# Key sums in two column runs, weight sums on one engine, and later output products in a fused attention and expert kernel

## The chip, the core and the metric

The kernel runs on one core of a Trainium2 chip. The core has TensorE (PE in the profile; PEld is its weight load), VectorE (DVE), ScalarE (ACT), GpSimd (POOL), SyncE (SP, which only issues transfers here) and 16 DMA engines. The metric is the time of one execution in microseconds (us) on the device. The kernel before takes 847.71 us, the median of three runs (847.57 to 850.11).

## The reference

An attention with a decay bias feeds one expert layer, and that feeds a second one. All arrays are float32.

```python
# 4 batches, 8 heads, 576 tokens, 64 wide
scores = scale * np.matmul(q, k.transpose(0, 1, 3, 2))
cum = np.cumsum(np.maximum(s, 0.0), axis=-1)
bias = -(cum[:, :, :, None] - cum[:, :, None, :])
scores = np.where(causal, -1000000000.0, scores + np.minimum(bias, 0.0))
attn = np.exp(scores - np.max(scores, axis=-1, keepdims=True))
attn = attn / (np.sum(attn, axis=-1, keepdims=True) + 1e-09)
x = np.matmul(attn, v)                       # to 2304 tokens x 512
h = np.maximum(x @ w_in, 0.0)                # first expert, 2048 wide
x = h * h @ w_out
h = np.maximum(np.maximum(x @ w1, x @ w2), x @ w3)   # second, 768 wide
return h @ w_out                             # w_out of the second expert
```

The running sum `cum` of the 32 rows of `s` (one row for each batch and head) is what the text below calls the key sums.

## The kernel before

**Setup.** The 32 rows of `s` are loaded into a tile `st`. VectorE clips and scales them (L581), scans them into running sums (L582), and cuts each sum into three bfloat16 parts that add up to it (L584 and L586, three casts with two subtractions between them). Each part goes by a small transfer into rows of two operand tiles: `ck` (three transfers from SP's queue) and `cq` (three from ACT's, L614). For the first pair of heads TensorE multiplies `xq` by `xk` (L644) and then adds `cq` by `ck` (L646) into the same bank, which puts the sums' difference into the scores. For the later pairs the parts go through `c_dram` (written at L588, read at L611). SP's queue then loads `xv` of pair 0 and all operands of the next pairs.

**Attention.** Sixteen pairs of heads run through nine units each: scores (L644 to L654), row maximum on VectorE (L667), exponential on ScalarE (L681), transposes on TensorE (L723), copies on ScalarE (L743 to L748), product with `xv` (L768). Meanwhile the expert weights, which are float64 words, are turned into two float32 halves. A job for one weight block loads its words (L392), works on them with VectorE (L397 to L408), adds two pieces (L415), rounds the high half on ScalarE (L429) and subtracts it for the low half (L433). The engine of L415 and L433 is `adder[0]`: POOL while attention runs, VectorE afterwards. `w_job` reads it once, when a job is made, so a job that begins in attention keeps POOL.

**First expert** (about 177 to 566 us). For each block of 128 hidden columns TensorE makes the hidden block (L812), ScalarE applies relu and square and rounds it (L971 to L973), VectorE makes the low half (L974), and two blocks later TensorE multiplies by `w_out` (L995).

**Second expert** (566 to 842 us). There are three groups of 768 tokens. A group has nine items, `m % PER` 0 to 8, of seven products each (L1132, places `c` 0 to 6 in an item), written so that an item's last products lie between the next item's first. ScalarE copies some product banks to tiles `s1`, `s5` and `s2` (L1033), VectorE adds others to them (L1051) and takes maxima (L1068, L1073) into `res`. After an item's last product `res` is ready; for output rows of 128 tokens `split_out` rounds it on ScalarE (L804) and takes the low half on VectorE (L807) into a tile `hh`, and `out_products` (L1104) multiplies by the second `w_out`: six such token blocks in a group, 18 products of 512 columns each, then a copy to `ob` (L1110 or L1112) and the store (L1114). `OUT2_AT` says after which item and which place of the next group each token block of the last group stands. The third group's blocks come at the end, one behind another. The order of all engines is the order of the code; weight tiles `sl` are a pool of 19, refilled from `keep_p` by SP (L504) when the last product on them is done.

Of the kernel before, what the change touches and what calls it, by code (L numbers as in the profile page):

```python
# [8 lines left out]
F32 = mybir.dt.float32  # L9
# [4 lines left out]
ALU = mybir.AluOpType  # L14
# [6 lines left out]
MAX_PAIRS = 0  # L21
PUMP_FROM = 9
PUMP_END = 0
PRE = 2
PRE_X = (30, 21, 12, 5)
PRE_AT = 1
# [17 lines left out]
FAR = 24  # L44
PACE_FAR = 3
RR = 2
OUT2_AT = {1: {0: 0, 4: 1}, 2: {1: 2, 5: 3}, 3: {0: 4, 2: 5}}
LAG = 2
MAX_OPEN = 3
ST_BUFS = 3  # L50
# [196 lines left out]
def kernel(  # L247
# [15 lines left out]
    nc = tc.nc  # L263
    P = 128
    D = v_tail.shape[2]
    S = qT.shape[2]
    H = 8
    BH = s.shape[0]
    B = BH // H
    NT, DM = out.shape  # L270
# [6 lines left out]
    NU = 2 * SQ // P + 1  # L277
# [6 lines left out]
    def f32(ap):  # L284
        return ap.bitcast(F32)
# [62 lines left out]
    T2 = 384  # L348
# [71 lines left out]
    def w_job(i, t):  # L420
        if i[0] == "P":
            return item_job(*i[1:])
        b = {}
        add = adder[0]
        first = words_of(i, b, lambda: (f32(b["a"]), add))

        def high_part():
            b["h"] = t[:, 0, :] if t is not None else sums_tile()[:, 0:512].bitcast(F32R)
            nc.scalar.copy(out=b["h"], in_=f32(b["a"]))  # L429

        def low_part():
            b["l"] = t[:, 1, :] if t is not None else b["a"].bitcast(F32R)
            add.tensor_tensor(out=b["l"], in0=f32(b["a"]), in1=f32(b["h"]), op=ALU.subtract)  # L433

        def store():
            for h, x in enumerate((b["h"], b["l"])):
                queue[0].dma_start(out=keep[i][:, h * 512:(h + 1) * 512], in_=f32(x))

        stages = first + [(high_part, 0, 0), (low_part, 1, 0.4)]
        takes, gives = {0: "st", 2: "wa"}, {6: ["st"], 8: ["wa"]}  # L440
        if t is None:
            stages += [(store, 1, 2), (lambda: None, 0, 0)]
            takes[7], gives[10], gives[8] = "sums", ["sums", "wa"], []
        return [x[0] for x in stages], takes, gives, tuple(zip(*[x[1:] for x in stages]))
# [107 lines left out]
    def setup():  # L552
# [3 lines left out]
        parts = st[2][0:BH, :].bitcast(BF16)[:, 0:3 * S].rearrange("p (r c) -> p r c", r=3)  # L556
        c8 = e_u[NU - 1][0:BH, 0:S]
        nc.sync.dma_start(out=sc, in_=s)
        k, q, cum, v = loads(0)
        k()  # L560
        q()
# [16 lines left out]
        nc.vector.memset(bound[:, 0:SQ - P], 0.0)  # L578
        nc.vector.memset(bound_l[:, 0:SQ], 0.0)
        nc.vector.memset(e_u[NU - 1][:, S:], 0.0)  # L580
        nc.vector.tensor_scalar(out=sc, in0=sc, scalar1=0.0, scalar2=8.0, op0=ALU.max, op1=ALU.mult)  # L581
        nc.vector.tensor_tensor_scan(out=c8, data0=one, data1=sc, initial=0.0, op0=ALU.mult, op1=ALU.add)  # L582
        for r in range(3):
            nc.vector.tensor_copy(parts[:, r, :], c8)  # L584
            if r < 2:
                nc.vector.tensor_tensor(out=c8, in0=c8, in1=parts[:, r, :], op=ALU.subtract)  # L586
        cum(parts)
        nc.sync.dma_start(out=c_dram, in_=parts)  # L588
        v()
        for j in range(2):  # L590
            nc.vector.tensor_copy(bound_l[rows(j), SQ:S], bound[rows(j), SQ - P + D * j:SQ - P + D * (j + 1)])

# [3 lines left out]
    def loads(p):  # L596
# [7 lines left out]
            nc.sync.dma_start(out=d["xq"], in_=qT[p])  # L604


        def cum(parts=None):
            for t, r, queue in ((ck[p % 3], 0, nc.sync), (cq[p % 3], 3, nc.sync if parts is None else nc.scalar)):
                if parts is None:
                    for j in range(2):  # L610
                        queue.dma_start(out=t[D * j + r:D * j + r + 3, :], in_=c_dram[2 * p + j])  # L611
                else:
                    for i in range(3):
                        queue.dma_start(out=t[r + i:r + i + D + 1:D, :], in_=parts[2 * p:2 * p + 2, i, :])  # L614

        def v():
            d["xv"] = hp.tile([P, 2, NKT, D], F32, tag="xv", name="xv")
# [261 lines left out]
    def experts():  # L879
# [138 lines left out]
        phS.close()  # L1018
        slots.soon_kept = SOON_KEPT_2
        with ExitStack() as ph2:  # L1020
            r_p, hh_p, c_p, s_p, o_p = (ph2.enter_context(tc.tile_pool(name=n, bufs=b, reuse_waits="tile"))
                                        for n, b in (("rr2", 2), ("hh2", 2), ("cc2", 1), ("ss2", 2), ("oo2", 2)))
            rings = dict(X=Ring(banks[0:3]), Z=Ring(banks[3:5]), Y=Ring(banks[5:6]))
            ring_o = Ring(banks[6:8])
            where = {0: "X", 1: "Z", 2: "X", 3: "Y", 4: "X", 5: "Z", 6: "X"}
# [3 lines left out]
            tmp = {}  # L1029

            def copied(m, name, bank):
                x = tmp[m, name] = s_p.tile([P, T2], F32, tag=name, name=name)
                nc.scalar.copy(out=x, in_=bank[:, 0:T2])  # L1033

            def after(m, i):
# [54 lines left out]
            def out_products(g, t, f, begin, end):  # L1090
# [5 lines left out]
                for k, (lo, hi) in enumerate(cols):  # L1096
# [8 lines left out]
                                                 start=(begin and n == h == c == 0),  # L1105
                                                 stop=(end and n == len(f) - 1 and h == 1 and c == 2))
                    if end:
                        ob = o_p.tile([P, DM], F32, tag="ob", name="ob")[:, 0:hi - lo]
                        if (t + k) % 2:
                            nc.vector.tensor_copy(ob, b)  # L1110
                        else:
                            nc.scalar.copy(out=ob, in_=b)  # L1112
                        ring_o.give(po.pop((g, t)))
                        nc.sync.dma_start(out=out[groups[g] + t * P:groups[g] + (t + 1) * P, lo:hi], in_=ob)  # L1114
# [3 lines left out]
            for item in main2:  # L1118
                if item[0] == "p":
# [23 lines left out]
                    if m == len(items) - 1 and i == 6:  # L1143
                        for t in range(2):
                            split_out(last, t, order2[-1:])
                else:
                    _, g, t, f, begin, end = item
                    out_products(g, t, f, begin, end)
                    ahead = t + (1 if g < last else 2)
                    if end and ahead < 2 * T2 // P:  # L1150
                        split_out(g, ahead, range(NQ))
                slots.pos += 1
# [64 lines left out]
```

## Time and profile before

| | |
|---|---|
| median of three runs | 847.71 us |
| the profiled execution, its own time | 847.02 us |
| its span | 845.2 us |
| TensorE busy | 826.4 us (98%) |
| VectorE, ScalarE, POOL busy | 524.3, 407.5, 175.4 us |
| granted TensorE clock | 1.00 throughout |
| attention, first expert, second expert | to 177, 177 to 566, 566 to 842 us |

The span is what the profiler saw between the first and the last instruction; 1.8 us of the execution lie around it. TensorE is busy nearly all the time, so the places to read are those where it waits, and those where the same run of products takes longer than elsewhere: the profile models the end of a matmul, so a short wait shows better in the distance between the starts than in the busy time.

### The profile page before, as it was taken

How to read it: one execution, taken by the hardware profiler on the slowest of the kernel's cores; microseconds unless marked ns; L12 is line 12 of the kernel's file. 1: busy time of each engine (PE TensorE's matmuls, PEld its weight loads, DVE VectorE, ACT ScalarE, POOL GpSimd, SP SyncE). 2: the span in 40 equal slices, each digit the busy share in tenths (PEclk: the TensorE clock that was granted, in tenths of full speed). 3: DMA queues.
4: the chain of work that ended last, by engine and by line, in shares of the span. 5: the costliest groups of instructions: out<-in, count | busy, mean ns of one | idle time of the engine just before them, and what ended most of it. 6: DMA issues, size and time to landing. Idle time of an engine off the chain costs nothing.

```text
span 845.2 us, 14494 instructions
## 1 busy us (share of the span) xinstructions
PE 826.4 (98%) x5284; PEld 700.5 (83%) x5284; DVE 524.3 (62%) x1103; ACT 407.5 (48%) x833; POOL 175.4 (21%) x273
## 2 busy tenths in 40 slices
PE   5999999999999999999999999999999999999998
PEld 3555565577888899999998888889998899899996
DVE  6777787749766656765877786843563335633442
ACT  5888889845544445445544555432242222421221
POOL 3054444544231323222123232100000000000000
PEclk9999999999999999999999999999999999999999
DMA  5565657453544454896758596639921573026602
GB/s 162 178 192 170 218 188 217 123 154 126 179 153 148 150 194 150 310 362 218 243 201 309 181 314 228 248 105 406 407 91 44 197 262 121 13 75 217 231 1 75
DMA packets 72631, 159.77 MB, mean 189 GB/s; under 512 B 12784, under 2 KB 32816, under 8 KB 72560
## 3 DMA queue, kind: packets, MB, share of 16 engines
q1 hardware_dynamic: 55764, 102.73, 36.1%
q0 software_dynamic: 16784, 56.11, 18.8%
q8 instruction: 41, 0.67, 0.3%
q14 instruction: 30, 0.25, 0.1%
q10 hardware_dynamic: 12, 0.01, 0.0%
HBM read 113.53 MB, written 45.27 MB: 188 GB/s over the span
## 4 chain that ended last, share of the span: by engine, by line
PE 91%; DVE 3%; ACT 2%; DMA 2%; POOL 1%; issue 0%; SPq 0%; DVEq 0%; ACTq 0%; POOLq 0%
PE banks L995 22%; PE banks L1132 13%; PE first L812 11%; PE banks L812 11%; PE banks L1104 9%; PE first L1132 8%; PE pairs L768 5%; PE pairs L723 3%; PE pairs L644 2%; PE pair L644 2%; PE pair L651 1%; ACT e L681 1%; DMA st<-in_w_in_dram 1%; PE pairs L651 1%; DVE hh L807 1%; PE pairs L646 1%
## 5 line engine op out<-in xcount | busy, mean ns | idle before, releaser
L995 PE MATMUL banks<-hh,sl 128*128 128x512 f32 (+1 forms) x960 | 210.1, 367 | 1.8 <-DVE hh L974 1.8
L995 PEld LDWEIGHTS banks<-hh,sl 128*128 128x128 f32 x960 | 175.1, 188 | 24.8 <-DVE hh L974 2.2
L1132 PE MATMUL banks<-xs,sl 128*128 128x384 f32 x702 | 131.2, 335 | 0.0
L1132 PEld LDWEIGHTS banks<-xs,sl 128*128 128x128 f32 x702 | 122.8, 188 | 0.9 <-DMA sl<-keep_p 0.2
L974 DVE TENSOR_TENSOR hh<-r,hh 128x512 fp32r<-128x512 f32 (+1 forms) x80 | 52.0, 651 | 98.8 <-ACT hh L973 98.6
L812 PE MATMUL first<-xs,sl 128*128 128x512 f32 (+1 forms) x432 | 93.6, 365 | 0.0
L812 PE MATMUL banks<-xs,sl 128*128 128x512 f32 (+1 forms) x432 | 93.6, 365 | 0.0
L681 ACT ACTIVATE e<-e,nm 128x128 f32<-128x128 f32 (+2 forms) x144 | 83.5, 585 | 10.0 <-DVE nm L667 9.9
L812 PEld LDWEIGHTS first<-xs,sl 128*128 128x128 f32 x432 | 78.6, 188 | 9.4
L812 PEld LDWEIGHTS banks<-xs,sl 128*128 128x128 f32 x432 | 78.6, 188 | 9.4
L1132 PE MATMUL first<-xs,sl 128*128 128x384 f32 x432 | 84.6, 335 | 0.3 <-DMA sl<-keep_p 0.3
L1104 PE MATMUL banks<-sl,hh 128*128 128x512 f32 (+1 forms) x342 | 78.4, 382 | 1.9 <-DVE hh L807 1.5
L1132 PEld LDWEIGHTS first<-xs,sl 128*128 128x128 f32 x432 | 75.8, 188 | 1.0 <-issue 0.6
L1104 PEld LDWEIGHTS banks<-sl,hh 128*128 128x128 f32 x342 | 61.4, 188 | 16.0 <-DVE hh L807 3.4
L971 ACT ACTIVATE r<-banks 128x512 f32<-128x512 f32 (+1 forms) x40 | 22.2, 556 | 91.6 <-PE banks L812 86.7
L971 ACT ACTIVATE r<-first 128x512 f32<-128x512 f32 (+1 forms) x40 | 22.2, 556 | 89.2 <-PE first L812 89.2
L1033 ACT COPY s<-first 128x384 f32<-128x384 f32 x36 | 17.2, 479 | 79.3 <-PE first L1132 79.2
L768 PEld LDWEIGHTS pairs<-et,xv 128*64 128x64 f32 (+1 forms) x448 | 27.8, 135 | 31.1 <-ACT e L681 8.9
L768 PE MATMUL pairs<-et,xv 128*64 128x320 f32 (+4 forms) x448 | 52.7, 367 | 0.0
L1033 ACT COPY s<-banks 128x384 f32<-128x384 f32 x45 | 21.6, 479 | 57.3 <-PE banks L1132 56.8
L972 ACT ACTIVATE r<-r 128x512 f32<-128x512 f32 (+1 forms) x80 | 47.2, 590 | 2.5
L973 ACT CAST hh<-r 128x512 fp32r<-128x512 f32 (+1 forms) x80 | 46.3, 579 | 2.5
(109 smaller groups left out, 1149.9 us busy)
## 6 DMA issues: line engine op xcount, KB each, us to landing
sl<-keep_p SPq DMA_DIRECT2D x68, 512.0 KB
st<-in_w_dram POOLq DMA_DIRECT2D x36, 256.0 KB, 5.7
st<-in_w_out_dram POOLq DMA_DIRECT2D x35, 256.0 KB, 3.9
sl<-keep_out SPq DMA_DIRECT2D x14, 512.0 KB
keep_p<-hi POOLq DMA_DIRECT2D x9, 768.0 KB, 5.2
keep_p<-sums POOLq DMA_DIRECT2D x9, 768.0 KB, 6.6
st<-in_w_in_dram POOLq DMA_DIRECT2D x22, 256.0 KB, 4.2
xk<-in_kT_dram SPq DMA_DIRECT2D x16, 288.0 KB
```

The costliest lines, as they stand in the source:

```text
L644: nc.tensor.matmul(b[:, j, 0:w], lhsT=d["xq"][rows(j), w - P:w], rhs=d["xk"][rows(j), 0:w], start=True, stop=False)
L681: nc.scalar.activation(out=e_u[u][:, 0:w], in_=e_u[u][:, 0:w], func=ACTF.Exp, scale=-1.0, bias=st.pop(n), accum_out=sums[p, win][:, col:co ...
L768: nc.tensor.matmul(pv[rows(j), f:(W0, W1)[w]], lhsT=xv[0:kr, j, k, :], rhs=rhs, start=(k == 0), stop=(k == last))
L812: nc.tensor.matmul(hps[:, 0:n], lhsT=w[:, wp, kk * P:(kk + 1) * P], rhs=x[kk][xp][:, 0:n], start=(kk == 0 and c == 0), stop=(kk == KD - 1 ...
L971: nc.scalar.activation(out=r[:, 0:n], in_=hps[:, 0:n], func=ACTF.Relu)
L972: nc.scalar.activation(out=r[:, 0:n], in_=r[:, 0:n], func=ACTF.Square)
L973: nc.scalar.copy(out=hh[:, 0, 0:n], in_=r[:, 0:n])
L974: nc.vector.tensor_tensor(out=hh[:, 1, 0:n], in0=r[:, 0:n], in1=f32(hh[:, 0, 0:n]), op=ALU.subtract)
L995: nc.tensor.matmul(xacc[d][:, 0:n], lhsT=w[:, wp, d * P:(d + 1) * P], rhs=hh[:, xp, 0:n], start=(m == 0 and c == 0), stop=(end and c == 2))
L1033: nc.scalar.copy(out=x, in_=bank[:, 0:T2])
L1104: nc.tensor.matmul(b, lhsT=hh[g, t][:, hp_, q, h, :], rhs=w[:, wp, lo:hi], start=(begin and n == h == c == 0), stop=(end and n == len(f) - ...
L1132: nc.tensor.matmul(at[m, b][:, 0:T2], lhsT=w[:, wp, at_w + kk * P:at_w + (kk + 1) * P], rhs=x[:, kk, xp, :], start=(i in (0, 1, 3) and kk ...
```

## The change

Three parts.

1. In the setup, the clip, the scan and the three parts are made for columns 0 to 383 and then for 384 to 575 (`sums_to`, twice). The second scan starts from the last sum of the first. Each part's two small transfers are issued as soon as that part is written, and the load of `xv` stands between the two runs. The second and third part come from two subtractions of the first instead of in place.
2. `w_job` reads `adder[0]` when an instruction is written, not when the job is made.
3. In the second expert, `OUT2_AT` moves the token blocks of the first two groups later and spaces them evenly; `hh` has three buffers instead of two; the third group's third block is split together with the first two, and each later one three blocks ahead. `s1`, `s5`, `s2` and `ob` share one ring of five tiles.

```diff
+FIRST_C = 384
-OUT2_AT = {1: {0: 0, 4: 1}, 2: {1: 2, 5: 3}, 3: {0: 4, 2: 5}}
+OUT2_AT = {1: {2: 0, 6: 1}, 2: {3: 2}, 3: {0: 3, 4: 4}, 4: {1: 5}}
...
-        add = adder[0]
-        first = words_of(i, b, lambda: (f32(b["a"]), add))
+        first = words_of(i, b, lambda: (f32(b["a"]), adder[0]))
...
-            add.tensor_tensor(out=b["l"], in0=f32(b["a"]), in1=f32(b["h"]), op=ALU.subtract)
+            adder[0].tensor_tensor(out=b["l"], in0=f32(b["a"]), in1=f32(b["h"]), op=ALU.subtract)
...
+        def sums_to(lo, hi, rest):
+            x, c, d = sc[:, lo:hi], c8[:, lo:hi], rest[0:BH, 0:hi - lo]
+            nc.vector.tensor_scalar(out=x, in0=x, scalar1=0.0, scalar2=8.0, op0=ALU.max, op1=ALU.mult)
+            nc.vector.tensor_tensor_scan(out=c, data0=one[:, lo:hi], data1=x, initial=c8[:, lo - 1:lo] if lo else 0.0,
+                                         op0=ALU.mult, op1=ALU.add)
+            nc.vector.tensor_copy(parts[:, 0, lo:hi], c)
+            cum(parts, 0, lo, hi)
+            nc.vector.tensor_tensor(out=parts[:, 1, lo:hi], in0=c, in1=parts[:, 0, lo:hi], op=ALU.subtract)
+            cum(parts, 1, lo, hi)
+            nc.vector.tensor_tensor(out=d, in0=c, in1=parts[:, 0, lo:hi], op=ALU.subtract)
+            nc.vector.tensor_tensor(out=parts[:, 2, lo:hi], in0=d, in1=parts[:, 1, lo:hi], op=ALU.subtract)
+            cum(parts, 2, lo, hi)
...
-        cum(parts)
-        nc.sync.dma_start(out=c_dram, in_=parts)
+        sums_to(0, FIRST_C, e_u[NU - 2])
         v()
+        sums_to(FIRST_C, S, e_u[NU - 3])
+        nc.sync.dma_start(out=c_dram, in_=parts)
...
-                                        for n, b in (("rr2", 2), ("hh2", 2), ("cc2", 1), ("ss2", 2), ("oo2", 2)))
+                                        for n, b in (("rr2", 2), ("hh2", 3), ("cc2", 1), ("ss2", 5)))
...
-                x = tmp[m, name] = s_p.tile([P, T2], F32, tag=name, name=name)
+                x = tmp[m, name] = s_p.tile([P, DM], F32, tag="s", name="s")[:, 0:T2]
...
-                        ob = o_p.tile([P, DM], F32, tag="ob", name="ob")[:, 0:hi - lo]
+                        ob = s_p.tile([P, DM], F32, tag="s", name="ob")[:, 0:hi - lo]
...
+                        split_out(last, 2, range(NQ))
...
-                    ahead = t + (1 if g < last else 2)
+                    ahead = t + (1 if g < last else 3)
```

How the instructions stand, at three places. First SP's queue at the setup; `ck_169` is pair 0's operand, `ck_170` and `cq_167` those of pair 1. Before:

```order
L604 DMA xq<-in_qT_dram 128x576
L614 DMA ck_169<-st 2x576 x3
L588 DMA c_dram<-st 32x1728
L618 DMA xv<-in_v_main_dram 128x2x256
L619 DMA xv<-in_v_tail_dram 64x2x64
L600 DMA xk<-in_kT_dram 128x576
L604 DMA xq<-in_qT_dram 128x576
L611 DMA ck_170<-c_dram 3x576 x2
L611 DMA cq_167<-c_dram 3x576 x2
```

The same queue with the change:

```order
L613 DMA xq<-in_qT_dram 128x576
L622 DMA ck_169<-st 2x384 x3
L626 DMA xv<-in_v_main_dram 128x2x256
L627 DMA xv<-in_v_tail_dram 64x2x64
L622 DMA ck_169<-st 2x192 x3
L598 DMA c_dram<-st 32x1728
L609 DMA xk<-in_kT_dram 128x576
L613 DMA xq<-in_qT_dram 128x576
L620 DMA ck_170<-c_dram 3x576 x2
L620 DMA cq_167<-c_dram 3x576 x2
```

Three transfers are added in front of `c_dram` and of all that pair 1 needs, and `xv` now goes ahead of them.

Second, POOL's queue at the step from attention to the first expert, from the last two products of attention rows (`ax`) on. Before:

```order
L786 TENSOR_TENSOR ax<-ax,px 128x320
L791 DMA x_at_75<-ax 128x320
L433 TENSOR_TENSOR sl_92<-wa,sl_92 128x512
L392 DMA st<-in_w_out_dram 128x512
L392 DMA st<-in_w_in_dram 128x512 x2
L415 TENSOR_TENSOR wa<-st 128x512 x2
L433 TENSOR_TENSOR sl_93<-wa,sl_93 128x512
L392 DMA st<-in_w_out_dram 128x512
L433 TENSOR_TENSOR sl_94<-wa,sl_94 128x512
L392 DMA st<-in_w_out_dram 128x512 x5
```

With the change:

```order
L794 TENSOR_TENSOR ax<-ax,px 128x320
L799 DMA x_at_75<-ax 128x320
L393 DMA st<-in_w_out_dram 128x512
L393 DMA st<-in_w_in_dram 128x512 x2
L393 DMA st<-in_w_out_dram 128x512 x6
```

POOL is left with issuing loads; its five sums stand on VectorE.

Third, TensorE in the second expert, from the product that is the last of the first group's ninth item (`banks_2999<-xs,sl_88` here) to the first token block (L1104). Before:

```order
L1132 MATMUL banks_2999<-xs,sl_88 128x384 x6
L1132 MATMUL banks_3002<-xs,sl_83 128x384 x6
L1132 MATMUL first_2885<-xs,sl_101 128x384 x6
L1104 MATMUL banks_3003<-sl_86,hh 128x512 x3
L1104 MATMUL banks_3003<-sl_96,hh 128x512 x3
```

With the change:

```order
L1140 MATMUL banks_3010<-xs,sl_88 128x384 x6
L1140 MATMUL banks_3013<-xs,sl_83 128x384 x6
L1140 MATMUL first_2896<-xs,sl_101 128x384 x6
L1140 MATMUL first_2895<-xs,sl_89 128x384 x6
L1140 MATMUL banks_3011<-xs,sl_87 128x384 x6
L1112 MATMUL banks_3014<-sl_86,hh 128x512 x3
L1112 MATMUL banks_3014<-sl_96,hh 128x512 x3
```

Four products stand between the item's end and the token block, where two stood. Every later token block of a group now also has four products ahead of it; before, the last of a group had two.

## Rows read from the trace of the kernel before

**Rows 1.** The page's part 1: busy time, share of the span and instructions by engine.
```profile
PE 826.4 (98%) x5284; PEld 700.5 (83%) x5284; DVE 524.3 (62%) x1103; ACT 407.5 (48%) x833; POOL 175.4 (21%) x273
```

**Rows 2.** Waits of TensorE, one of them: us in total, times, longest.
```profile
PE pairs L646 <- DMA cq<-st: 4.7, 1, 4.7
```

**Rows 3.** Chain that ended last, setup: start us, us, what.
```profile
2.70 0.71 DVE st L581
3.43 1.35 DVE e L582
4.81 0.53 DVE st L584
...
6.86 0.76 DVE e L586
...
8.31 1.76 DMA cq<-st
...
10.42 0.29 PE pairs L646 x2
```

**Rows 4.** Timeline, VectorE, first pair: start us, us, engine line operation.
```profile
14.01 0.55 DVE L667 CUSTOM_DVE_ANT_0 e<-pairs,bound 128x384 f32<-128x384 f32 x1
...
16.61 0.76 DVE L667 CUSTOM_DVE_ANT_0 e<-pairs,bound_l 128x576 f32<-128x576 f32 x1 [0.34 <-PE pairs L654]
```

**Rows 5.** Timeline, SP and TensorE, first two pairs.
```profile
12.51 0.55 SPq L611 DMA_DIRECT2D cq<-c_dram  x2
...
14.42 0.39 PE L646 MATMUL pair<-ck,cq 64*128 64x512 bf16 x2
...
17.05 0.22 PE L646 MATMUL pair<-ck,cq 64*128 64x128 bf16 x2
```

**Rows 6.** Timeline, step from attention to first expert; idle time and releaser in brackets.
```profile
183.38 1.30 POOL L433 TENSOR_TENSOR sl<-wa,sl 128x512 fp32r<-128x512 f32 x1
...
184.61 0.56 POOL L392 DMA_DIRECT2D st<-in_w_out_dram  x1
...
188.37 0.43 DVE L397 TENSOR_SCALAR wa<-st 128x512 uint32<-128x512 uint32 x1 [2.06 <-DMA st<-in_w_out_dram]
...
190.79 1.04 POOL L415 TENSOR_TENSOR wa<-st 128x512 f32<-128x512 f32 x1 [3.36 <-DVE st L408]
...
192.39 0.59 ACT L971 ACTIVATE r<-first 128x512 f32<-128x512 f32 x1
...
193.74 1.89 DVE L974 TENSOR_TENSOR hh<-r,hh 128x512 fp32r<-128x512 f32 x1
...
195.68 2.79 PE L995 MATMUL banks<-hh,sl 128*128 128x512 f32 x11 [1.82 <-DVE hh L974]
...
197.34 0.68 DVE L974 TENSOR_TENSOR hh<-r,hh 128x512 fp32r<-128x512 f32 x1
```

**Rows 7.** Stretches of the second expert: start:end, length, busy us by engine, clock, DMA.
```profile
636.11:642.40 6.29, 5.72 (x25) 4.37 (x25) 1.79 (x3) 1.31 (x2) 0.00 (x0) 1.00 0.00 0
645.54:650.71 5.17, 5.17 (x26) 4.43 (x26) 0.56 (x1) 1.21 (x2) 0.00 (x0) 1.00 0.01 3
675.65:680.17 4.52, 4.41 (x20) 3.32 (x19) 0.92 (x2) 0.48 (x1) 0.00 (x0) 1.00 1.00 333
646.59:650.71 4.12, 4.12 (x20) 3.38 (x20) 0.00 (x0) 1.21 (x2) 0.00 (x0) 1.00 0.02 4
```

**Rows 8.** Timeline, second expert: the split of a first token block, and the last group's blocks.
```profile
636.51 0.83 ACT L804 CAST hh<-res 128x768 fp32r<-128x768 f32 x1 [1.76 <-DVE res L1073]
637.38 0.96 DVE L807 TENSOR_TENSOR hh<-res,hh 128x768 fp32r<-128x768 f32 x1 [0.90 <-ACT hh L804]
...
818.58 6.20 PE L1104 MATMUL banks<-sl,hh 128*128 128x512 f32 x25
...
825.27 16.62 PE L1104 MATMUL banks<-sl,hh 128*128 128x512 f32 x89 [0.49 <-DVE hh L807]
```

**Rows 9.** Waits of SP's queue for a weight tile to come free.
```profile
SPq L504 <- PE first L1132: 17.3, 8, 5.9
```

More of the change, by code (lines that the diff above doesn't have):

```diff
@@ L580, in setup @@
         nc.vector.memset(e_u[NU - 1][:, S:], 0.0)
[L581 to L586, printed above, removed]
-        cum(parts)
+        sums_to(0, FIRST_C, e_u[NU - 2])
+        v()
+        sums_to(FIRST_C, S, e_u[NU - 3])
         nc.sync.dma_start(out=c_dram, in_=parts)
-        v()
         for j in range(2):
@@ L604, in q_all, with cum @@
             nc.sync.dma_start(out=d["xq"], in_=qT[p])
-        def cum(parts=None):
+        def cum(parts=None, i=0, lo=0, hi=S):
             for t, r, queue in ((ck[p % 3], 0, nc.sync), (cq[p % 3], 3, nc.sync if parts is None else nc.scalar)):
@@ L612, in cum @@
                 else:
-                    for i in range(3):
-                        queue.dma_start(out=t[r + i:r + i + D + 1:D, :], in_=parts[2 * p:2 * p + 2, i, :])
+                    queue.dma_start(out=t[r + i:r + i + D + 1:D, lo:hi], in_=parts[2 * p:2 * p + 2, i, lo:hi])
         def v():
@@ L1020, in experts @@
         with ExitStack() as ph2:
-            r_p, hh_p, c_p, s_p, o_p = (ph2.enter_context(tc.tile_pool(name=n, bufs=b, reuse_waits="tile"))
-                                        for n, b in (("rr2", 2), ("hh2", 2), ("cc2", 1), ("ss2", 2), ("oo2", 2)))
+            r_p, hh_p, c_p, s_p = (ph2.enter_context(tc.tile_pool(name=n, bufs=b, reuse_waits="tile"))
+                                        for n, b in (("rr2", 2), ("hh2", 3), ("cc2", 1), ("ss2", 5)))
             rings = dict(X=Ring(banks[0:3]), Z=Ring(banks[3:5]), Y=Ring(banks[5:6]))
```

## Prediction, written before the changed kernel was run

> **What bounds the kernel now.** I read the page's busy times first. TensorE works for 826.4 of 845.2 us [rows 1], at full clock throughout, and the change takes no matmul away. So it can only give back time in which TensorE waits, and there are some 19 us of that. Next I read TensorE's waits, and then, at each place that the diff touches, the timeline around the wait: what ended last there. There are three kinds of place.
>
> First, the setup. TensorE starts pair 0's score products and then waits 4.7 us for `cq` [rows 2]. The chain is VectorE alone: clip, scan, three casts and two subtractions from 2.70 to 8.28, then one transfer and its pick-up, and the product at 10.42 [rows 3]. Second, the step to the first expert: at 195.68 TensorE has stood 1.82 us for the low half of a hidden block [rows 6]. Third, the token blocks of the second expert, where the wait itself looks like 0.5 us but the stretch is longer: six small products and 18 large ones take 6.29 us at the first block of a group and 5.17 us at the second [rows 7].
>
> **Part 1, the setup.** For 384 instead of 576 columns I scale by what VectorE shows for one form at both widths: 0.55 against 0.76 us [rows 4], a factor of 0.72. The first run is a clip of 0.51, a scan of 0.97, a cast of 0.38 and three subtractions of 0.55, 3.5 us, with five gaps of 0.03 some 3.65 us, from 2.70 to 6.35. Before, the last part was ready at 8.28, and the product came 2.14 us later [rows 3]; so it comes at 8.5 instead of 10.42, a gain of 1.9. At the ends: if the instructions shrank in proportion (0.67) it would be 2.1; if they did not shrink at all, six of them would still end sooner than seven, at some 7.7, for a gain of 0.6. I take 1.9, since the width rows are the same engine's.
>
> What it costs: the second run is six shorter instructions, about 2.2 us, so VectorE is free for pair 0's first maximum at about 8.9, 0.1 to 0.2 after it could start. The second run's parts are written by 8.6, and SP's queue, with `xv` ahead, should have issued them by 9.7, to land before 12; they are first wanted by the 512-wide product, at 14.42 [rows 5], so at 12.5 with the shift. That is covered, with little left. SP has three more issues in front of `c_dram` (two such take 0.55 us [rows 5]), and `c_dram` can only be written after the second run; so pair 1's `cq`, which is read from there and was issued at 12.51, will be issued at 12.5 to 13, while its first user, at 17.05, moves to 15.1 [rows 5]. Before, 4.5 us lay between; then 2 to 2.5, about the 2.14 that a small transfer takes [rows 3]. I take off 0.2 for VectorE and 0.1 for this, and keep **1.6 us**, with 0 to 2.1 as the ends. Nothing in attention makes the engines wait for the clock on the wall: their waits are for each other, so a shift at its start should come through to its end.
>
> **Part 2, the weight sums.** Five additions leave POOL and cost VectorE five times about 0.68 [rows 6], 3.4 us over some 15. The chain to the wait is this: POOL does a low half until 184.6 and only then issues the load of `w_out` words; VectorE has them at 188.37; after four operations POOL adds them at 190.79 to 191.83; ScalarE, waiting in order for that sum, can start on the hidden block only at 192.39; VectorE then takes 1.89 us for its low half instead of 0.68 [rows 6]. With the change the load is issued at 183.4, 1.2 sooner; the sum is 0.68 instead of 1.04; so the hidden block is rounded some 1.6 us sooner, by 192.7, and its low half ends at 193.4 if VectorE takes 0.68. TensorE's wait began at 193.86 (195.68 less 1.82), so it is gone: **1.7 us**, with 0.7 and 2.0 as ends. At the lower end the load lands no sooner, since the loads behind it compete; then only POOL's slow sum and the slow low half are saved.
>
> Here VectorE's 1.89 us lie under POOL's next sum, and 0.68 is the same form with POOL only issuing [rows 6]. The Trainium skill (SBUF — State Buffer, Who interferes with whom) says that a VectorE instruction with two inputs in SBUF and a GpSimd instruction that reads SBUF exclude each other for a whole instruction. By that rule moving the sums also frees VectorE of such stops, and the wait goes; without it VectorE would only have more to do, which is the third rival.
>
> **Part 3, token blocks.** First block of a group: `hh` is rounded from 636.51 and ready at 638.34 [rows 8], while TensorE could have begun the block at 637.15 (636.11 and six products as long as those at 645.54). The loss is 6.29 less 5.17, 1.12 us [rows 7], in two groups. Two more products ahead of the block are 2 us, so it begins at 639.2, 0.9 after `hh`. Last block of a group: 4.52 against 4.12 us [rows 7], 0.40, also twice; two products stood ahead of it, and four will; the way from a block's end through the output copy, the rounding and the subtraction is about 2.4 us, against 4.2. At the end of the kernel the third block waits for its `hh`, because the second buffer comes free only when the first block is done: 25 products from 818.58 should put the next at 824.3, and it starts at 825.27 [rows 8], 0.97 late. With a third buffer that split follows the others some 3 us ahead of its use. Together 2.24, 0.80 and 0.97, **4.0 us**. The ends are 2.5 (one block of each group still waits) and 4.1.
>
> The blocks' later places keep the second `w_out` tiles longer, so the next group's weights come later; the tiles are ordered up to 14 steps ahead of use (`SOON_KEPT_2`), so I cost that at nothing. The shared ring is five tiles for what had eight; a tile returns after five allocations, which is never less than eight products and one block, 12 us. Also nothing, but it is the rival on the other side.
>
> **Sum.** 1.6, 1.7 and 4.0 are 7.3 us. Against the profiled execution's 847.02 that is 839.7; the median of the runs lies 0.7 above that execution, and half of this goes into the forecast: **840.0 us**.
>
> **Rivals.** (a) The setup's gain is given back. Pair 1 waits for its own `cq`, because SP's queue and the loads ahead of it move less than TensorE does. For it: 2.14 against 2 to 2.5 us; and the first loads fill the DMA engines. Against it: `xv` has gone ahead into a stretch where they idled. It costs 1 to 1.6 us and gives 841.5. The Trainium skill (DMA: Bandwidth & Descriptors, Queues, rings and completion order) says that a transfer's completion write lands only after every earlier write of the same DMA engine, across its queues. By that rule pair 1's `cq` would land behind `xk` and `xq`, issued just before it, and this rival would be the likely one; no row here shows a landing.
>
> (b) The step to the expert keeps a wait: VectorE, with 3.4 us more, is late with the hidden block itself. If its low half still took 1.89, and the two sums stand in front of it, 1.4, against 1.2 from the earlier load, TensorE waits 2.0 instead of 1.8. That gives 841.9.
>
> (c) The token blocks wait for something else at their new places, half of the 4.0 stays, 842.0.
>
> (d) Slower. ScalarE's product copies wait for output stores, now that both use one ring: a tile is freed when its store has landed, and stores stand in SP's queue behind weight loads that wait up to 5.9 us [rows 9]. With 3 us for the store that is 9, under the 12 of above. From 12 us on, each of the twelve blocks in the first two groups costs what is over; slower than before needs more than 7.3 us in all, 0.6 us each with everything else as forecast, or a store that lands after 12.6. At 1 us each the time is 852.
>
> (e) The change does not do what it says: the early pieces do not help because the first product still waits for all of `cq`, and the two other parts hold. 841.6.
>
> **How the numbers follow.** Forecast 0.60; (a) 0.15; (b) 0.07; (c) 0.07; (d) 0.03; (e) 0.02; two of (a) to (c) together 0.06, at 843.5. About 0.3%, 2.5 us, is what a measurement of this kernel tells from no change. All but (d) lie more than that under 847.7, but the profile can hide a wait that takes over; faster 0.90, same 0.07, slower 0.03. The forecast's own ends are 838.8 (all three at their best) and 842. The range reaches to (a), (b), (c) and the pair: 838.6 to 843.6.
>
> **What will show it.** In the profile after: pair 0's first `cq` product at about 8.5 and pair 1's without a wait; no wait of TensorE between 170 and 200 us from attention's end, with VectorE's low half at 0.7; the stretch of a first token block at 5.2 us instead of 6.3, a last one at 4.1; the last run of token blocks without a break. I am wrong if TensorE's wait for `cq` comes back at pair 1, if the hidden blocks still wait for ScalarE behind a rounding, or if ScalarE's copies in the second expert wait for a store.

## The result and the profile after

The changed kernel takes 839.99 us (median of 4 runs, 838.92 to 843.16) against 847.86 us for the kernel before in the same session: a ratio of 0.990, 95% interval 0.9877 to 0.9923. The forecast was 840.0. The profiled execution took 840.53 us with a span of 838.7, so the span lost 6.5 us. In the profile after, a line number is mostly that of before plus 8: L644 is L652, L646 is L654, L974 is L982, L995 is L1003, L1104 is L1112.

Page of the changed kernel, part 1 (first), and its list of TensorE's waits (us in total, times, longest):

```profile
PE 825.0 (98%) x5284; PEld 701.2 (84%) x5284; DVE 524.3 (63%) x1113; ACT 407.9 (49%) x833; POOL 169.1 (20%) x268
```

```profile
PE pairs L652 <- DMA xq<-in_qT_dram: 4.9, 1, 4.9
PE pairs L654 <- DMA cq<-st: 2.9, 1, 2.9
...
PE first L1140 <- ACT s L1041: 0.5, 1, 0.5
```

The wait for `cq` is 2.9 instead of 4.7 [rows 2]; those for hidden blocks and token blocks are gone from the list. One line is new, 0.5 us at the second expert's first products. In the kernel before the same product stands still as well, for a weight tile; from the first product of that expert to the place after the wait it is 6.86 us before and 7.10 after, so 0.24 us are lost there. ScalarE's copy, which the line names, had itself waited for TensorE and not for a store. Waits of 0.18 and 0.72 us stand at this place in two kernels whose second expert is the old one (e2_sums and e1_setup below), so the 0.24 lies within what differs from execution to execution.

Timeline of the changed kernel, setup, TensorE (start us, us, engine, line, operation):

```profile
8.61 0.29 PE L654 MATMUL pairs<-ck,cq 64*128 64x128 bf16 x2 [2.93 <-DMA cq<-st]
...
8.66 1.19 PE L652 MATMUL pair<-xk,xq 64*128 64x256 f32 x4
...
11.65 2.04 PE L652 MATMUL pair<-xk,xq 64*128 64x512 f32 x4
...
13.47 0.64 PE L654 MATMUL pair<-ck,cq 64*128 64x512 bf16 x2
...
16.35 0.22 PE L654 MATMUL pair<-ck,cq 64*128 64x128 bf16 x2
...
17.89 0.65 PE L652 MATMUL pairs<-xk,xq 64*128 64x256 f32 x4
```

The first product comes at 8.61 instead of 10.42 [rows 3], 1.81 sooner; pair 1's first at 16.35 instead of 17.05 [rows 5], 0.70 sooner. So 1.1 us of the gain seem to go in pair 0, at its 512-wide products. That is the question of the first experiments.

Timeline of the changed kernel, step to the first expert:

```profile
182.63 0.54 POOL L393 DMA_DIRECT2D st<-in_w_out_dram  x1
...
188.22 0.43 DVE L398 TENSOR_SCALAR wa<-st 128x512 uint32<-128x512 uint32 x1 [3.35 <-DMA st<-in_w_out_dram]
...
191.22 0.42 DVE L398 TENSOR_SCALAR wa<-st 128x512 uint32<-128x512 uint32 x1
...
191.67 0.69 DVE L402 SCALAR_TENSOR_TENSOR st<-st,wa 128x512 uint32<-128x512 uint32 x1
...
192.28 0.68 DVE L982 TENSOR_TENSOR hh<-r,hh 128x512 fp32r<-128x512 f32 x1
...
192.68 3.14 PE L1003 MATMUL banks<-hh,sl 128*128 128x512 f32 x12
```

The low half takes 0.68 instead of 1.89 [rows 6], and the twelve products run in 3.14 us, with some 0.3 us of standing left in them.

Timeline of the changed kernel, second expert: first and last token block of a group, and the last group's run of blocks:

```profile
635.81 1.20 PE L1140 MATMUL banks<-xs,sl 128*128 128x384 f32 x6
636.85 4.28 PE L1112 MATMUL banks<-sl,hh 128*128 128x512 f32 x18
640.97 1.23 PE L1140 MATMUL banks<-xs,sl 128*128 128x384 f32 x6
...
678.38 4.28 PE L1112 MATMUL banks<-sl,hh 128*128 128x512 f32 x18
682.50 2.27 PE L1140 MATMUL banks<-xs,sl 128*128 128x384 f32 x12
...
813.16 22.19 PE L1112 MATMUL banks<-sl,hh 128*128 128x512 f32 x114
```

Six small products and a first block take 640.97 less 635.81, 5.16 us instead of 6.29; a last block 4.12 instead of 4.52 [rows 7]. The last group's 114 products run without a break in 22.19 us; before, the same stretch went from 818.58 to 841.89 [rows 8], 23.31.

### The profile page after: what moved, and what is told of

It reads as the page before. It is cut to its first block, busy times and chain, and to the rows that moved or that the text cites. A ratio compares the mean times of both kernels' runs of the same rounds, so it can differ in the third digit from the quotient of the medians.

```text
span 838.7 us, 14515 instructions
## 1 busy us (share of the span) xinstructions
PE 825.0 (98%) x5284; PEld 701.2 (84%) x5284; DVE 524.3 (63%) x1113; ACT 407.9 (49%) x833; POOL 169.1 (20%) x268
## 4 chain that ended last, share of the span: by engine, by line
PE 97%; ACT 1%; DVE 1%; DMA 0%; issue 0%; DVEq 0%
PE banks L1003 24%; PE banks L1140 15%; PE first L820 12%; PE banks L820 12%; PE first L1140 9%; PE banks L1112 9%; PE pairs L776 6%; PE pairs L731 3%; PE pairs L652 2%; PE pair L652 2%; PE pair L659 1%; PE pairs L659 1%; PE pairs L654 1%; PE pairs L779 1%; PE pair L654 1%; ACT e L689 0%
## 5 line engine op out<-in xcount | busy, mean ns | idle before, releaser
L1003 PE MATMUL banks<-hh,sl 128*128 128x512 f32 (+1 forms) x960 | 210.1, 367 | 0.0
L1003 PEld LDWEIGHTS banks<-hh,sl 128*128 128x128 f32 x960 | 175.1, 188 | 22.9 <-DVE hh L982 0.4
L982 DVE TENSOR_TENSOR hh<-r,hh 128x512 fp32r<-128x512 f32 (+1 forms) x80 | 50.9, 636 | 96.9 <-ACT hh L981 96.7
L1112 PE MATMUL banks<-sl,hh 128*128 128x512 f32 (+1 forms) x342 | 76.5, 379 | 0.0
L1112 PEld LDWEIGHTS banks<-sl,hh 128*128 128x128 f32 x342 | 61.7, 188 | 11.5
L1059 DVE TENSOR_TENSOR c<-banks,s 128x384 f32<-128x384 f32 x45 | 25.0, 555 | 42.9 <-PE banks L1140 42.7
```

Of the source, the lines that this page charges most:

```text
L982: nc.vector.tensor_tensor(out=hh[:, 1, 0:n], in0=r[:, 0:n], in1=f32(hh[:, 0, 0:n]), op=ALU.subtract)
L1003: nc.tensor.matmul(xacc[d][:, 0:n], lhsT=w[:, wp, d * P:(d + 1) * P], rhs=hh[:, xp, 0:n], start=(m == 0 and c == 0), stop=(end and c == 2))
L1112: nc.tensor.matmul(b, lhsT=hh[g, t][:, hp_, q, h, :], rhs=w[:, wp, lo:hi], start=(begin and n == h == c == 0), stop=(end and n == len(f) - ...
```

## The experiments

Twelve further kernels ran. In the table, "mark" is the start of TensorE's second run of twelve products by `w_out`, about the end of attention; "step wait" is TensorE's wait at the step to the first expert. All but the median are of the one profiled execution; "not listed" means that its list of waits has no such line.

| kernel | median us (before, same session) | first cq product | pair 1's first | mark | step wait |
|---|---|---|---|---|---|
| before | 847.86 | 10.42 | 17.05 | 182.60 | 1.82 |
| changed | 839.99 (847.86) | 8.61 | 16.35 | 181.80 | not listed |
| e1_setup | 846.95 (848.14) | 8.61 | 16.50 | 181.82 | 2.36 |
| e2_sums | 846.16 (848.14) | 10.43 | 17.96 | 183.64 | 0.53 |
| e3_blocks | 843.69 (848.14) | 10.44 | 17.65 | 183.00 | 2.29 |
| e4_xv_last | 840.07 (848.14) | 8.60 | 15.89 | 181.23 | not listed |
| w_before | 848.15 (847.89) | 10.43 | 15.84 | 181.48 | 2.82 |
| w_after | 839.67 (847.89) | 8.69 | 14.94 | 180.76 | 0.77 |
| w_xv | 839.93 (847.89) | 8.67 | 15.82 | 182.77 | 0.34 |
| e5_low_pool | 841.42 (847.89) | 8.61 | 16.27 | 181.47 | 1.00 |
| e6_sum_pool | 840.63 (848.98) | 8.61 | 16.03 | 181.79 | 0.36 |
| e7_places | 841.09 (848.98) | 8.60 | 15.75 | 181.32 | not listed |
| e8_third_hh | 842.75 (848.98) | 8.61 | 15.82 | 181.01 | 1.07 |
| best | 839.02 (848.98) | 8.65 | 14.28 | 180.09 | 0.20 |

**One part at a time.** The diff of each is that part of the change alone, on the kernel before.

```diff
# e1_setup: sums_to in two runs, xv between them
# e2_sums: adder[0] read when an instruction is written
# e3_blocks: OUT2_AT, three hh buffers, shared ring, earlier splits
```

> The setup part alone, put into the kernel before. Theory Q (SP's queue): the first cq product starts at about 8.6 instead of 10.42, but pair 0's 512-wide one waits for the second run's ck, which SP issues behind xv; it starts at about 13.5, pair 1's first at 16.3 to 16.4, and the second expert's first product moves from 565.7 to 564.9: 0.8 us, a time of about 847.0. Rival, the prediction as written: pair 1's first cq product at 15.4, the second expert 1.6 us sooner, 846.2. If the parts depend on each other the setup alone gives less than 0.4 us.

> The move of the weight sums to VectorE alone. Theory X (VectorE stopped beside POOL): the subtraction of the low half before TensorE's wait takes 0.68 instead of 1.89 us, the job's fourth operation 0.69 instead of 1.67, the wait of 1.82 shrinks to under 0.3; the second expert starts 1.8 to 1.9 us sooner, a time of about 846.0. Rival L, the prediction's own chain (earlier load, shorter sum, ScalarE free sooner): the w_out load lands about 1.2 us sooner than at 188.4, and the hidden block is rounded by ScalarE within 1 us of TensorE's need. Under both the gain is near 1.8; what tells them apart is where the load lands and when ScalarE has rounded the block.

> The part in the second expert alone. If the parts are independent: nothing changes up to 565.7 (within 0.1), a first token block with the six products ahead of it takes 5.2 instead of 6.3 us, a last one 4.1 instead of 4.5, the last group's run of blocks 22.2 instead of 23.3; 3.8 to 4.1 us in all, a time of about 843.8. Rival: part of the gain of the three parts together is only there because the weights' loads or the first expert ends sooner; then this part alone gives under 3.4 us.

The medians fall by 1.19, 1.98 and 4.45 us, 7.6 in all, against 7.87 together: the parts add up within what the times can tell, since each median is known to 1 or 2 us. Ratios: 0.9971 (0.9948 to 0.9995), 0.9969 (0.9954 to 0.9983), 0.9937 (0.9915 to 0.9959). The times came as expected (847.0, 846.0 and 843.8), e1's 13.48 and 16.50 us for its two products about as theory Q had them, and e3's stretches too (5.16, 4.12 and 22.19 us). Two places did not: e2 still waits 0.53 us at the step instead of under 0.3, and the second expert's first product came at 566.95 in e1 instead of 564.9 and at 566.58 in e3 instead of 565.7. And pair 1 told something unforeseen: e2 and e3 have the setup of before unchanged, and yet pair 1 comes 0.9 and 0.6 us later than in the profile of before. e2's 512-wide products (first fence) beside the same ones of the kernel before (second):

```profile
13.48 2.03 PE L643 MATMUL pair<-xk,xq 64*128 64x512 f32 x4
...
17.96 0.22 PE L645 MATMUL pair<-ck,cq 64*128 64x128 bf16 x2
```

```profile
13.47 1.13 PE L644 MATMUL pair<-xk,xq 64*128 64x512 f32 x4
```

One setup, one start, 2.03 and 1.13 us. So the profile of before had caught a good execution, and the 0.70 read from the two traces is not the part's effect.

**Is it the queue?** I had thought that the 512-wide product waits for the second run's `ck`, issued behind `xv`.

```diff
-        v()
         sums_to(FIRST_C, S, e_u[NU - 3])
         nc.sync.dma_start(out=c_dram, in_=parts)
+        v()
```

> The changed kernel, with the load of xv behind the second column run and behind the write of c_dram, where it stood in the kernel before. Theory Q: SP issues the last ck of the second run at about 8.9 instead of 9.8; pair 0's 512-wide cq product starts at 12.4 to 12.7 instead of 13.47, pair 1's first at 15.1 to 15.4 instead of 16.35; the second expert starts 1.0 to 1.2 us sooner, a time of about 839.0. Rival S (the twelve small transfers themselves are what lasts, each waiting for an earlier one's completion): 13.4 and 16.3 stay, the time is the changed kernel's within 0.3. Rival P (the prediction's first rival): the 512-wide product comes sooner, but pair 1 waits for its own cq and stays at 15.8 or later.

The 512-wide `cq` product came at 13.26, only 0.21 sooner, and the median is 840.07. In e7 and e8 below, with `xv` between the two runs, it came at 13.12 and 13.19, so theory Q fell. The median is as S has it, but e2 points to the pace of TensorE, so the next three runs keep TensorE busy in the setup.

**TensorE at work before its first product.** Products of zeros into a bank that is used later; where w_before has 17 of them, w_after and w_xv have 10:

```diff
+    def idle_products(n):
+        z = bound.bitcast(BF16)
+        for _ in range(n):
+            nc.tensor.matmul(pairs[0][:, 0, :], lhsT=z[:, 0:P], rhs=z[:, 0:512], start=True, stop=True)
...
+        if n == 0:
+            idle_products(6)
...
+            if n == 0:
+                idle_products(17)
```

> The kernel before, with products of zeros on TensorE while it waits in the setup: six 512 wide ahead of the first score product and 17 between that and the first cq product; no output reads them. In the runs so far the same form (four products 256 wide) took 1.19 us as pair 0's second and 0.65 later, and the fast pace began 3.0 to 5.7 us after the first cq product, at another place in each execution: 512-wide products of 1.13, 1.71 and 2.03 us with one and the same setup. Theory C (TensorE works at the slow pace until it has been busy for a while, and that is why the traces before and after show a shift of 0.7 where 1.8 came at the first product): here pair 0's 256-wide xk products take about 0.65 and the 512-wide ones 1.1; pair 1's first cq product comes at 16.2 to 16.9, and its distance to that of the changed kernel with the same products is 1.5 to 1.8 us. Theory Q (the second column run's ck arrives late behind xv): the distance is 0.7 to 1.0.

> The changed kernel with the same products of zeros, six and ten. Theory C: first cq product at 8.6, pair 0's 256-wide products 0.65, its 512-wide cq product at about 12.0 instead of 13.47, pair 1's first at 14.7 to 15.3 instead of 16.35; the time 1.0 to 1.6 us under the changed kernel's, 838.7. Theory Q: the 512-wide cq product still waits for its ck till 13.2 or later and pair 1 stays at 16.0 or later, whatever the pace; the time stays at 840. If the zeros cost something at their end, the first cq product comes later than 8.7.

> The changed kernel with the products of zeros and with xv's load behind the second column run and c_dram. With xv last alone pair 0's 512-wide cq product moved only from 13.47 to 13.26. Theory C: nothing more to gain, pair 1's first cq product within 0.2 of that of the changed kernel with the zeros alone. Theory Q: 0.8 to 1.3 us sooner than there. The prediction's first rival: pair 1's cq, which SP issues at 13.4 here instead of 13.0, is now waited for; pair 1's first cq product at 15.5 or later, after the other's.

Timelines of w_before (first) and w_after (second):

```profile
10.43 0.23 PE L655 MATMUL pairs<-ck,cq 64*128 64x128 bf16 x2 [1.24 <-DMA cq<-st]
10.49 0.67 PE L651 MATMUL pair<-xk,xq 64*128 64x256 f32 x4
...
12.30 1.08 PE L651 MATMUL pair<-xk,xq 64*128 64x512 f32 x4
13.21 0.39 PE L655 MATMUL pair<-ck,cq 64*128 64x512 bf16 x2
```

```profile
8.74 0.67 PE L659 MATMUL pair<-xk,xq 64*128 64x256 f32 x4
...
10.56 1.08 PE L659 MATMUL pair<-xk,xq 64*128 64x512 f32 x4
11.47 0.38 PE L663 MATMUL pair<-ck,cq 64*128 64x512 bf16 x2
...
14.57 0.49 PE L659 MATMUL pair<-xk,xq 64*128 64x128 f32 x4 [0.59 <-DVE sm L708]
14.94 0.40 PE L663 MATMUL pair<-ck,cq 64*128 64x128 bf16 x2
```

Theory C holds: the 256-wide products take 0.67 instead of 1.19, the 512-wide ones 1.08 instead of 2.04, and the `cq` product behind them starts 1.74 us apart in the two kernels, so all of the setup's gain is there, and `ck` was never late, which puts S out as well. Where I missed: pair 1 comes at 15.84 in w_before, ahead of the forecast 16.2, and is only 0.90 apart, and w_after's median is 839.67 instead of 838.7, not to be told from the changed kernel's (ratio 0.9892, 0.9869 to 0.9916). In w_after TensorE stands 0.59 us ahead of pair 1, and in w_xv, with pair 1's loads issued still later, longer and for a load by name:

```profile
15.47 0.49 PE L659 MATMUL pair<-xk,xq 64*128 64x128 f32 x4 [1.36 <-DMA xq<-in_qT_dram]
...
18.16 1.17 PE L659 MATMUL pairs<-xk,xq 64*128 64x256 f32 x4
```

The profile puts w_after's 0.59 us down to VectorE's `sm`, but in best, below, that step starts at 14.50, after pair 1's first product at 13.97, so the product does not need it. SP issued `xq` 3.22 us ahead of the product in w_after (11.35) and 3.30 in w_xv (12.17), which fits one cause for both. So once TensorE is fast, pair 1 waits for its own `xq`: the prediction's rival (a) in another transfer, and only there. w_before's time did not fall although its mark is early; that belongs to the step below.

**The step to the first expert, half by half.**

```diff
# e5_low_pool, on the changed kernel
+        add = adder[0]
-            adder[0].tensor_tensor(out=b["l"], ...
+            add.tensor_tensor(out=b["l"], ...
# e6_sum_pool: add in words_of instead
```

> The changed kernel, with the subtraction of a job's low half back on the engine read when the job is made: two of them stand on POOL again at the step to the first expert, the three additions stay on VectorE. The load of w_out words is then issued about 1.2 us later, behind the first of them. Theory X+L (both the later load and VectorE's slow steps beside POOL cost): VectorE's fourth operation takes 1.2 to 1.7 and the hidden block's low half 1.7 to 1.9 us, and TensorE waits 2.5 to 3.2 us. Load alone (VectorE keeps 0.69): a wait of 1.2 to 1.6. Sum alone (the addition on VectorE is what helped): no wait over 0.3. The time follows: 842.5 to 843.5, 841.3, or 840.

> The changed kernel with the additions of a job made in attention back on POOL and only the low halves' subtractions on VectorE: the other half of e5_low_pool. By theory X+L the load is issued 0.8 us after the mark (the second twelve products by w_out), as in the changed kernel, not 2.0; VectorE's one slow step is the second one of the next block, 1.4 instead of 0.69, beside POOL's sum, which VectorE in turn has not to make; the wait of TensorE is that of the changed kernel, 0 to 0.8 us, and so is the time. If the additions are what costs: a wait of 1 to 2 us.

Timeline of e5_low_pool:

```profile
191.61 1.51 POOL L434 TENSOR_TENSOR sl<-wa,sl 128x512 fp32r<-128x512 f32 x1 [3.18 <-ACT sl L430]
...
191.90 1.78 DVE L983 TENSOR_TENSOR hh<-r,hh 128x512 fp32r<-128x512 f32 x1
...
193.73 2.81 PE L1004 MATMUL banks<-hh,sl 128*128 128x512 f32 x11 [1.00 <-DVE hh L983]
```

The low half takes 1.78 us again, under POOL's subtraction, and TensorE waits 1.00. The wait is shorter than forecast because the load landed 3.87 us after its issue; in 12 of the 14 executions it took 5.4 to 6.8 (3.76 in the kernel before). "Landed" is read here, and below, from VectorE's first step on the words, which comes within 0.2 us of the profile's own landing. With the changed kernel's 5.59 the wait would by estimate have been 2.7 (1.00 and the 1.72 between), as forecast. The other slow step that was forecast did not come (0.69 at 191.29), and the median, 841.42, lies under the forecast 842.5. The "load alone" price is the nearest to the wait, but it does not fit VectorE's row. From the landing to TensorE's product it is 6.37 us here, 5.13 in e6, and 4.8 in each kernel with all sums on VectorE that waits (e2, w_after, w_xv, e8, best); what their waits differ by is the landing: e8's 1.07 has the latest, 6.78. In e6 VectorE's slow step did not come, since its words arrived when POOL's sum was over, and the load is issued 1.0 us after the mark, not 2.0. So the subtraction, not the addition, is the half that matters. This is read from the traces: the medians, 841.42 and 840.63, are of two sessions, and the intervals of the ratios overlap (0.9894 to 0.9948 and 0.9875 to 0.9927).

The whole chain is best read in e1_setup, which has the changed setup and POOL's sums, and whose mark is the changed kernel's (181.82 and 181.80). Its timeline, and a stretch (start:end, length, busy by engine, clock, DMA):

```profile
182.61 1.31 POOL L434 TENSOR_TENSOR sl<-wa,sl 128x512 fp32r<-128x512 f32 x1
...
183.84 0.56 POOL L393 DMA_DIRECT2D st<-in_w_out_dram  x1
...
189.59 0.43 DVE L398 TENSOR_SCALAR wa<-st 128x512 uint32<-128x512 uint32 x1 [4.06 <-DMA st<-in_w_out_dram]
...
192.31 1.41 DVE L402 SCALAR_TENSOR_TENSOR st<-st,wa 128x512 uint32<-128x512 uint32 x1
...
193.64 1.75 DVE L983 TENSOR_TENSOR hh<-r,hh 128x512 fp32r<-128x512 f32 x1
...
195.45 4.26 PE L1004 MATMUL banks<-hh,sl 128*128 128x512 f32 x11 [2.36 <-DVE hh L983]
```

```profile
195.40:197.00 1.60, 1.55 (x4) 1.27 (x5) 1.57 (x2) 0.75 (x2) 1.60 (x2) 0.50 0.44 143
```

Against the changed kernel the load is issued 1.21 us later and lands 1.37 later; from its landing to TensorE it is 5.86 us, 1.06 more than 4.8. Together 2.4, about the length of the wait. The 1.06 is the low half's 1.75 for 0.68: POOL's addition stops VectorE's step as well, 1.41 for 0.69, but that is about what the addition costs VectorE when it makes it itself (0.69). And after the wait the granted clock is 0.50, the lower level, 1.2 GHz: the eleven products take 4.26 us instead of 2.79 in the kernel before [rows 6], 1.5 us more. In w_before the same came after a wait of 2.82 us (4.38 us for the eleven), and that ate the gain of its early mark in this execution. Of its ten executions five have a mean granted clock of 0.997 or 0.998 and take 848.39 to 848.95 us; the other five read 1.000 and take 845.54 to 847.90. So the clock's fall is one reason at least that its ratio is 0.9991 (0.9978 to 1.0005).

**The second expert, half by half.**

```diff
# e7_places, on the changed kernel: hh 2 buffers, old rings, old splits
# e8_third_hh, on the changed kernel
-OUT2_AT = {1: {2: 0, 6: 1}, 2: {3: 2}, 3: {0: 3, 4: 4}, 4: {1: 5}}
+OUT2_AT = {1: {0: 0, 4: 1}, 2: {1: 2, 5: 3}, 3: {0: 4, 2: 5}}
```

> The changed kernel with the token blocks at their new places, but two buffers of hh, the old rings for product copies and stores, and the old splits of the last group. If the two halves of the part are independent: first and last token blocks of a group as in the changed kernel (5.2 and 4.1 us with what is counted with them), the last run of blocks again with a break, 23.3 instead of 22.2 us, 1.1 us more in all. Rival: with two buffers the later places give nothing, since a split waits for the buffer of the block two before; then the first groups lose up to 3 us as well and a wait for hh shows in them.

> The changed kernel with the third buffer, the shared ring and the earlier splits, but the token blocks of the first two groups at their old places. If the halves are independent: the last run of blocks 22.2 us without a break, the first block of a group 6.3 and the last 4.5 us as in the kernel before, 3.0 us more than the changed kernel in all. Rival: the third buffer alone removes the waits in the first two groups too, and the time is the changed kernel's.

Timelines of e7_places (first) and e8_third_hh (second):

```profile
818.95 16.64 PE L1112 MATMUL banks<-sl,hh 128*128 128x512 f32 x89 [0.49 <-DVE hh L815]
```

```profile
635.11 0.50 PE L1112 MATMUL banks<-sl,hh 128*128 128x512 f32 x1
636.10 4.19 PE L1112 MATMUL banks<-sl,hh 128*128 128x512 f32 x17 [0.49 <-DVE hh L815]
...
816.18 22.19 PE L1112 MATMUL banks<-sl,hh 128*128 128x512 f32 x114
```

In the traces the halves are independent. With two buffers only the last group's break is back; with the old places only the waits in the first two groups are. The medians are 1.1 and 2.8 us over the changed kernel's, but they are of another session, and the times do not confirm the first: against the kernel before of their own session e7 gains 7.89 us, as much as the changed kernel's 7.87, and e8 6.23; the intervals of all three ratios overlap (e7 0.9917, 0.9887 to 0.9946; e8 0.9931, 0.9911 to 0.9952).

**A version with both findings.** The zeros, with `xk` and `xq` of pair 1 between the two runs, `xv` behind `c_dram`:

```diff
-        v()
+        rest_1 = loads(1)
+        for f in rest_1[:2]:
+            f()
         sums_to(FIRST_C, S, e_u[NU - 3])
         nc.sync.dma_start(out=c_dram, in_=parts)
+        v()
...
+        return rest_1[2:]
```

> The changed kernel with the products of zeros, with xk and xq of pair 1 loaded between the two column runs and xv behind c_dram. With the zeros alone, pair 1 waited 0.59 us for its xq, and with xv last for 1.36 us. Theory (pair 1's own loads set its start once TensorE is at the fast pace): first cq product 8.65, pair 1's first at 14.0 to 14.3 without a wait ahead, 0.6 to 0.9 us sooner than with the zeros alone, and a time of 838.8 to 839.2. If the time of attention is set by other engines from pair 1 on, pair 1 starts sooner but the end of attention stays within 0.3. If the earlier xk and xq delay the second run's ck, pair 0's 512-wide cq product starts after 11.8.

Timeline of best, pair 1's first products:

```profile
13.97 0.44 PE L663 MATMUL pair<-xk,xq 64*128 64x128 f32 x4
14.28 0.40 PE L667 MATMUL pair<-ck,cq 64*128 64x128 bf16 x2
```

Pair 1 starts without a wait, 0.66 us sooner than with the zeros alone and 1.56 sooner than w_before; the mark, 180.09, is the earliest of all. The median is 839.02 and the ratio 0.9878 (0.9857 to 0.9900): better than the changed kernel's by the trace, but the two intervals overlap, so the times don't show it.

## Why the prediction was right, and where it was not

**Setup, 1.6.** The first product was forecast at 8.5 and came at 8.61. The pair of profiles keeps 0.70 of the 1.81, but over executions without zeros the mark is 183.08 on average with the old setup (three) and 181.54 with the changed one (the changed kernel, e1, e5, e6, e7, e8): 1.5 us. The term was right in size. Pair 1's first `cq` product was forecast at 15.1 and came at 15.75 to 16.50 in these six. What the working lacked is TensorE's pace: rows of one execution of before were taken for the kernel's own. "Covered, with little left" held for `ck`, and rival (a) showed only where TensorE was made faster. Rival (e) is out: the early pieces do start the first product.

**Step to the expert, 1.7.** The pair of profiles gives 1.85: 2.65 by the second expert's first product, less 0.80 at the mark. The cause was put down half wrongly. I had the hidden block late because ScalarE rounds it behind the weights' sum. Three more rows of the trace of the kernel before show that it was not:

```profile
184.18 0.62 ACT L973 CAST hh<-r 128x512 fp32r<-128x512 f32 x1
...
191.69 0.43 DVE L397 TENSOR_SCALAR wa<-st 128x512 uint32<-128x512 uint32 x1 [0.98 <-DMA st<-in_w_in_dram]
...
192.15 1.67 DVE L401 SCALAR_TENSOR_TENSOR st<-st,wa 128x512 uint32<-128x512 uint32 x1
```

ScalarE had rounded the block that TensorE waits for by 184.80, nine microseconds ahead of its low half at 193.74 [rows 6]; the rounding that begins at 192.39 is of a later block, and ends after that low half has begun. The low half came late because it stands in VectorE's order behind two steps of the next weight job, which waited there for `w_in` words, and because it and one of those steps were stopped beside POOL. From the first of the two steps to the end of the low half it is 3.94 us (191.69 to 195.63), and 1.74 in the changed kernel (191.22 to 192.96); the two stopped instructions, 1.67 and 1.89 instead of 0.69 and 0.68, are 2.19 of the 2.20 between. That first step stands 9.09 us behind the mark before and 9.42 after, so 0.33 is given back: 1.87, the whole of the 1.85. The low half's 1.89 was named, but as the last link only. The load's 1.2 us was right as a step (1.21 in e1) and gave nothing in this pair, since in the profile of before the load landed 3.76 us after its issue and in the changed one 5.59. The waits with POOL's sums are 1.82 (before) and 2.3 to 2.8 (e1, e3, w_before), and those with all sums on VectorE 0 to 1.1, so the term was a little small, more so with the clock's fall.

Rival (b), VectorE as the bound, did not come at its price, since the low half takes 0.68. But the wait that is left is VectorE's: in the changed kernel its eight steps from the load's landing to the low half's end fill 188.22 to 192.96 without a break. The rule of the Trainium skill (SBUF — State Buffer, Who interferes with whom), that a VectorE instruction with two inputs in SBUF and a GpSimd instruction that reads SBUF exclude each other, agrees with these traces: 1.75 to 1.89 us for the low half with POOL at a subtraction, 0.68 without.

**Token blocks, 4.0.** Measured 1.13 and 0.40 in the group shown, 1.15 and 0.38 in the next one, and 1.12 at the end: 4.2, less the 0.24 at the expert's first products. The fifth block of a group, too, had two products ahead of it, and lost nothing (4.13 us at 669.42), so it was not the two products alone that made the last one wait; what else did was not tried. The spans leave 3.85 (6.5 less 2.65), near enough. Rivals (c) and (d) did not come; no wait for a store shows.

**The sum.** 7.3 was forecast from the profiled execution; the medians differ by 7.87 and the parts alone by 7.6. The profiled pair differs by 6.5, since its setup keeps 0.70. That 839.99 meets 840.0 so closely is luck: the four executions lie between 838.92 and 843.16.

## What to carry to other kernels

Before a stage's gain is read from two profiles, read the same stage in a few executions that leave it unchanged: here a start-up differed by 0.9 us and one load by up to 3. A step moved off a second engine can pay on the first one, if the two stop each other and a waited-for result stands behind both in order. And whoever speeds a start must look at the next wait in line: here the second pair's loads.

## What the runs showed of the hardware

- TensorE's first products run at about half pace: four 256-wide ones 1.19 us against 0.65 at 17.89. The fast pace came at different points of the same program (512-wide products of 1.13, 1.71 and 2.03 us with one setup), and in the kernels with zeros from 1.93 us on it was there at the first `cq` product. The clock column reads 1.00 in these stretches, so this is read from durations alone; that it is the clock's lower level is likely, not shown.
- Later the column does show it. In w_xv, after the wait of 1.36 us:

```profile
14.10:15.40 1.30, 0.01 (x2) 0.00 (x0) 0.72 (x4) 1.30 (x4) 0.00 (x0) 1.00 0.81 248
...
17.00:18.00 1.00, 1.00 (x20) 0.76 (x18) 0.38 (x2) 0.09 (x1) 0.00 (x0) 0.50 0.94 339
...
20.00:21.00 1.00, 1.00 (x14) 0.61 (x14) 0.36 (x4) 0.89 (x2) 0.00 (x0) 1.00 0.93 278
```

  The clock fell after waits of 1.36, 2.36 and 2.82 us (w_xv, e1, w_before) and not after 1.82 and 2.29 (before, e3), so the length of the wait alone does not decide it; what does stays open here. From pair 1's first `cq` product to the mark it is 166.95 us in w_xv and 165.19 to 165.82 in the thirteen others: by estimate the fall there cost 1.1 to 1.8 us.
- A 256 KB load of weight words landed 3.8 to 6.8 us after its issue at the same place of the program, read in the same way; why was not tried.
